# Scaling v by batch: the pair maxima taken apart, and the lanes' maximum through a diagonal and a product of ones

## The chip, the core and the metric

The kernel runs on one core of one Trainium2 chip. Its engines work side by side, each through its own queue in order: TensorE (PE: matmuls, with the weight loads counted apart as PEld), VectorE (DVE), ScalarE (ACT), GpSimd (POOL) and SyncE (SP), which here only issues transfers. The metric is the time of one execution in device microseconds.

## The reference

Causal attention over 8 batches of 8 heads, 576 positions, 64 channels a head, with a bias from cumulative sums; then a feed-forward network (FFN) 512 to 2048 to 512 over all 4608 tokens. q and k come multiplied by 8.

```python
def _attn_ref(q, k, v, s):                      # q, k, v: [8, 8, 576, 64]
    scores = matmul(q, k.transpose(0, 1, 3, 2)) / sqrt(64)
    cum = cumsum(maximum(s, 0), axis=-1)
    bias = -(cum[:, :, :, None] - cum[:, :, None, :])
    scores = where(causal, -1e9, scores + minimum(bias, 0))
    attn = softmax(scores)                      # over the last axis
    return matmul(attn, v)

def _moe_ref(x, w_in, w_out):                   # x: [4608, 512]
    h = x @ w_in                                # [4608, 2048]
    g = where(h >= 1, h, where(h <= -1, 0, (h + 1) ** 2 / 4))
    return g @ w_out
```

## The kernel before, in words

**Tiling.** Heads go in pairs: pair n = 4 * batch + p, with p from 0 to 3. A pair's queries go in two halves, 0 to 319 (query tiles 0 to 2) and 320 to 575 (tiles 3 and 4), and a pair's half is a job. The eight jobs of a batch are the first halves of its four pairs and then the second halves. Tiles are named by pair: `s21_0_1_0` is a score bank of pair 21, tile 0, head 1, from key column 0; `h4_0_9` is block 9 (of 0 to 15) of the FFN's hidden layer for batch 4's first half. Below, "job 19" is the job of pair 19 that the place in question shows.

**A job** has eight slots k. In slot 0 the operands of its scores are made: q and k are split in a high and a low part, Q1s and K1s, Q2s and K2s, by three copies on ScalarE (L392 to L394) and two subtractions on VectorE (L395, L396). These tiles have one buffer each, so a job's operands wait for the scores of the job in front. From slot 2 on come six units of scores: two products on TensorE (L446, L447) into one of two banks of PSUM that all `s` and `px` tiles share, a pass on VectorE (L452: adds the mask, writes p, and keeps the running minimum mn in a second small instruction), and the exponential on ScalarE (L463). The weights are then normalized and split in two float16 parts: sums and reciprocal rs (L502, L503, VectorE), GpSimd (L507, L509, L510), ScalarE (L508), VectorE (L513), and turned by a transposing transfer on SP's queue (L514, pt<-pb). In slot 7 the job in front is finished: thirty products with v into px (L555), and x is split from px by ScalarE (L572) and VectorE (L573).

**FFN steps** of the half whose attention is done (the first half's in a batch's second four jobs, the second half's in the next batch's first four) stand between the slots. A step takes 12 products for a block of h (L614, 320 or 256 columns), ScalarE's evacuation u (L626), two of VectorE (L629, L630), g in two parts (L640 ScalarE, L641 GpSimd), and the products y (L653), two steps later. "FFN products" below are those of L614 and L653.

**Scaling v.** v is loaded a batch ahead into four buffers (`load_v`, slot 1 of the sixth job, of the seventh in the first batch) and scaled by a power of two taken from the batch's largest |v|. `batch_start(b)` finds it: four maxima of 128 x 640 (L295), the maximum of the four (L297), then the maximum over the 128 lanes: a transposing product into a row (L110), VectorE's maximum of the row on one lane (L112), a floor to a power of two in two steps (L95, L96), a cast (L118), a product of ones that spreads it to all lanes (L120), and a copy out of PSUM (L121). A reciprocal and a multiply make rc (L304, L305). GpSimd scales v with rc for each pair of the new batch (L403, slot 1 of the pair's first job); the low part follows on VectorE. Before, `batch_start(b)` is called whole, in slot 5 of the last job of batch b - 1.

**What sets the order.** The Python code gives a program order; a scheduler simulates a timeline and writes each engine's queue from it. `tc.high_priority(offset)` brings instructions forward in its choice (the passes have `TTR_LEAD` = 10000, the FFN's evacuations 6000), and `tc.issue_after(x)` keeps an instruction behind x. So an edit in one place can move others. The first four jobs and the load and split of the weights make the startup, some 130 us in which no steady order holds.

Of the kernel before, what the change touches and what calls it, by code (L numbers as in the profile page):

```python
# [7 lines left out]
BF16 = mybir.dt.bfloat16  # L8
F16 = mybir.dt.float16
F32 = mybir.dt.float32  # L10
# [5 lines left out]
ALU = mybir.AluOpType  # L16
AX = mybir.AxisListType.X
# [3 lines left out]
B, H, S, D = 8, 8, 576, 64  # L21
DM, DFF = 512, 2048
P = 128
NPAIR = H // 2
# [10 lines left out]
TINY = 2.0 ** -50  # L35
# [9 lines left out]
TTR_LEAD = 10000  # L45
# [26 lines left out]

V_K = 5


@with_exitstack
def attention_ffn(ctx: ExitStack, tc: tile.TileContext, qT, kT, vn, s, w_in, w_out, yT):
    nc = tc.nc
    LOADQ, CUMQ, FIRSTQ = nc.sync, nc.scalar, nc.sync
    V, A, G, T = nc.vector, nc.scalar, nc.gpsimd, nc.tensor  # L80

    cp = ctx.enter_context(tc.tile_pool(name="cp", bufs=1))
    ap = ctx.enter_context(tc.tile_pool(name="ap", bufs=2))
    gp = ctx.enter_context(tc.tile_pool(name="gp", bufs=2))
    dp = ctx.enter_context(tc.tile_pool(name="dp", bufs=1, space=DRAM))
    ps_s = ctx.enter_context(tc.tile_pool(name="ps_s", bufs=2, space=PSUM))
    ps_h = ctx.enter_context(tc.tile_pool(name="ps_h", bufs=2, space=PSUM))
# [6 lines left out]
    def pow2floor(out, in_, least):  # L94
        V.tensor_scalar(out, in_, least, None, ALU.max)  # L95
        V.tensor_scalar(out.bitcast(I32), out.bitcast(I32), 0x7F800000, None, ALU.bitwise_and)  # L96

    ident = cp.tile([P, P], F32, name="ident")
# [5 lines left out]
    ones = cp.tile([P, P], BF16, name="ones")  # L104
    G.memset(ones, 1.0)

    def column_max(src, name, bank=(ps_s, "s")):

        row = bank[0].tile([P, 512], F32, tag=bank[1], name=f"row_{name}")
        T.transpose(row[:1, :P], src, ident)  # L110
        top = ap.tile([P, 1], F32, tag="top", name=f"top_{name}")
        V.tensor_reduce(top[:1], row[:1, :P], axis=AX, op=ALU.max)  # L112
        return top[:1]

    def spread(dst, top, name, bank=(ps_s, "s")):

        t16 = ap.tile([P, 1], BF16, tag="t16", name=f"t16_{name}")
        V.tensor_copy(t16[:1], top)  # L118
        col = bank[0].tile([P, 512], F32, tag=bank[1], name=f"col_{name}")
        T.matmul(col[:, :1], ones[:1], t16[:1], start=True, stop=True)  # L120
        V.tensor_copy(dst, col[:, :1])  # L121

    def lane_sum(dst, src, name, tag):

# [157 lines left out]
    vraw, csc, rcs, exs, hsc, rsc, usc, wsc, ubi, gsc, ysc, msc = ({} for _ in range(12))  # L282

    def load_v(b):
        for p in range(NPAIR):
            v = vraw[b, p] = ap.tile([P, NB, P], F32, tag="vraw", bufs=4, name=f"v{b}_{p}")
            G.memset(v[TAIL:, NB - 1], 0.0)
            nc.sync.dma_start(v[:, :NB - 1], vn[b, p, :SP - P].rearrange("(j p) n -> p j n", p=P))
            nc.sync.dma_start(v[:TAIL, NB - 1], vn[b, p, SP - P:])

    def batch_start(b):
        c = ap.tile([P, NPAIR], F32, tag="csc", name=f"c{b}")
        for p in range(NPAIR):
            v = vraw[b, p].rearrange("p j n -> p (j n)")
            V.tensor_reduce(c[:, p:p + 1], v, axis=AX, op=ALU.max, apply_absolute_value=True)  # L295
        t = ap.tile([P, 1], F32, tag="mt", name=f"mt{b}")
        V.tensor_reduce(t, c, axis=AX, op=ALU.max)  # L297
        bank = (ps_h, "h") if b == 1 else (ps_s, "s")
        top = column_max(t, f"m{b}", bank)
        pow2floor(top, top, TINY)  # L300
        m = msc[b] = ap.tile([P, 1], F32, tag="mb", name=f"mb{b}")
        spread(m, top, f"m{b}", bank)
        r = rcs[b] = ap.tile([P, 1], F32, tag="rcs", name=f"rc{b}")
        V.reciprocal(r, m)  # L304
        V.tensor_scalar(r, r, 4096.0, None, ALU.mult)  # L305
# [41 lines left out]
    def plain(n, hf):  # L347
        return jobs.index((n, hf)) < PLAIN_JOBS
# [4 lines left out]
    def att_load(n, hf):  # L353

        b, h0 = n // NPAIR, 2 * (n % NPAIR)
        q0, N, _ = HALF[hf]
        W = q0 + N
        if whole(n, hf):
            for t, src, c0 in zip(operands(n, hf), (qT, kT), (q0, 0)):
                sv = src[b, h0:h0 + 2, :, c0:W].rearrange("h d n -> d h n")  # L360
                (FIRSTQ if jobs.index((n, hf)) < FIRST_N else LOADQ).dma_start(t[:D, :, :W - c0], sv)
            return
        rq = ap.tile([P, 2, N], F32, tag="rq", bufs=1, name=f"rq{n}_{hf}")
        rk = ap.tile([P, 2, W], F32, tag="rk", bufs=1, name=f"rk{n}_{hf}")
        for t, src, c0 in ((rq, qT, q0), (rk, kT, 0)):
            sv = src[b, h0:h0 + 2, :, c0:W].rearrange("h d n -> d h n")
            for d0 in (0, D):
                (FIRSTQ if jobs.index((n, hf)) < FIRST_N else LOADQ).dma_start(t[d0:d0 + D], sv)
        raws[n, hf] = rq, rk

    def att_prep(n, hf):

        q0, N, _ = HALF[hf]
        W = q0 + N
        cd = cumd[2 * n:2 * n + 2].rearrange("h l n -> l h n")
        if not whole(n, hf) and not split_tiles:
            split_tiles.extend(operand_tiles(F32R, "s"))
            constant_rows(*split_tiles[1])
        Qc, Kc = operands(n, hf) if whole(n, hf) else split_tiles[1]
        if jobs.index((n, hf)) < CH_N:  # L380
            for hd in range(2):
                r = ch[2 * n + hd:2 * n + hd + 1]
                CUMQ.dma_start(Qc[D:D + 2, hd, :N].bitcast(F32), r[:, :, q0:W].bitcast(F32))
                CUMQ.dma_start(Kc[D + 2:D + 4, hd, :W].bitcast(F32), r[:, :, :W].bitcast(F32))
        else:
            CUMQ.dma_start(Qc[D:D + 2, :, :N].bitcast(F32), cd[:, :, q0:W])
            CUMQ.dma_start(Kc[D + 2:D + 4, :, :W].bitcast(F32), cd[:, :, :W])
        if whole(n, hf):
            return
        rq, rk = raws.pop((n, hf))  # L390
        (Q1, K1), (Q2, K2) = split_tiles
        A.copy(Q1[:, :, :N], rq)  # L392
        A.copy(K1[:, :, :W], rk)
        A.copy(Q2[:D, :, :N], rq[:D])  # L394
        V.tensor_tensor(Q1[D:, :, :N], rq[D:], Q1[D:, :, :N].bitcast(F32), ALU.subtract)  # L395
        V.tensor_tensor(K2[:D, :, :W], rk[:D], K1[:D, :, :W].bitcast(F32), ALU.subtract)  # L396

    def v_prep(n):

        b, p = n // NPAIR, n % NPAIR  # L400
        v, r = vraw.pop((b, p)), rcs[b]
        VT = vts[n] = ap.tile([P, 2, NB, P], F16, tag="vt", bufs=5, name=f"vt{n}")
        G.tensor_scalar(VT[:, 0], v, r, 1.0, ALU.mult, ALU.mult)  # L403
        if n < V_POOL:
            G.tensor_scalar(v, v, r, 1.0, ALU.mult, ALU.mult)
            G.tensor_tensor(VT[:, 1], v, VT[:, 0], ALU.subtract)
        vbs[n] = VT, v, r

    def v_low(n):
        VT, v, r = vbs.pop(n)  # L410
        if n >= V_POOL:
            with tc.issue_after(ttr[0]):
                V.scalar_tensor_tensor(VT[:, 1], v, r, VT[:, 0], ALU.mult, ALU.subtract)
# [3 lines left out]
    ttr = [None]  # L417
# [157 lines left out]
    jobs = [(NPAIR * b + p, hf) for b in range(B) for hf in range(2) for p in range(NPAIR)]  # L575

    def att_slot(j, k):

        if j < len(jobs):
            n, hf = jobs[j]  # L580
            if k == 0:
                att_prep(n, hf)
            if plain(n, 0):
                if k in (1, 4) and hf == 1 and j < PLAIN_JOBS + 2:
                    v_prep(2 * (j - PLAIN_JOBS) + k // 4)
            elif hf == 0 and k == 1:
                v_prep(n)
            elif hf == 0 and k == V_K:
                v_low(n)
            if k >= 2:  # L590
                scores(n, *UNITS[hf][k - 2])
            if k == 3 and j + 1 < len(jobs):
                att_load(*jobs[j + 1])
            if k == 1 and j % (2 * NPAIR) == V_J + (j < 2 * NPAIR) and j // (2 * NPAIR) + 1 < B:
                load_v(j // (2 * NPAIR) + 1)
            if k == 5 and j + 1 < len(jobs) and jobs[j + 1][0] % NPAIR == 0 and jobs[j + 1][1] == 0:
                with tc.issue_after(ttr[0]):
                    batch_start(jobs[j + 1][0] // NPAIR)
        if k == OUT_K and 1 <= j <= len(jobs) and j != NPAIR:
            while j == len(jobs) and late:  # L600
                late.pop(0)()
            att_out(*jobs[j - 1])
# [109 lines left out]
    c = 0  # L712
    for t in range(8 * NPAIR):
        if t % W1_SLOTS == 0:
            w1_task(c)
            c += 1
        if t == 2:
            load_v(0)
        if t == 6:
            batch_start(0)  # L720
            rc0 = cp.tile([P, 1], F32, name="rc0")
            V.tensor_scalar(rc0, rcs[0], 2.0 ** -10, None, ALU.mult)
        att_slot(t // 8, t % 8)
# [17 lines left out]
    t = 8 * NPAIR  # L741
    for j in range(16 * NP):
# [14 lines left out]
        else:  # L757
# [3 lines left out]
            m = 2 * (j // 8 % 2)  # L761
# [36 lines left out]
```

## Time and profile before

| | us |
|---|---|
| median of three runs | 1073.28 (1072.75 to 1077.13) |
| profiled execution, its own time | 1077.62 |
| its span in the profile | 1075.7, at a mean granted clock of 0.989 |

Each row of the page's first part gives an engine's busy time, its share of the span and its instructions. A row of the stages gives the stretch in us from the span's start, its length, the busy time of PE, PEld, DVE, ACT and POOL with their instructions, the granted TensorE clock, the DMA share and the transfers' rate in GB/s. A row of waits tells who waited <- for which engine's tile and line: us in total, times, longest. A row of the timeline gives start, length, engine, line, operation, output<-inputs, shapes, and how many like instructions it stands for; in brackets how long the engine was idle before it and what ended that. A row with two colons gives the least, median and largest duration in ns, the first and the last start in us, and the shapes.

### The profile page before, as it was taken

How to read it: one execution, taken by the hardware profiler on the slowest of the kernel's cores; microseconds unless marked ns; L12 is line 12 of the kernel's file. 1: busy time of each engine (PE TensorE's matmuls, PEld its weight loads, DVE VectorE, ACT ScalarE, POOL GpSimd, SP SyncE). 2: the span in 40 equal slices, each digit the busy share in tenths (PEclk: the TensorE clock that was granted, in tenths of full speed). 3: DMA queues.
4: the chain of work that ended last, by engine and by line, in shares of the span. 5: the costliest groups of instructions: out<-in, count | busy, mean ns of one | idle time of the engine just before them, and what ended most of it. 6: DMA issues, size and time to landing. Idle time of an engine off the chain costs nothing. (4 is left out here: it accounts for less than half of the span.)

```text
span 1075.7 us, 25023 instructions
## 1 busy us (share of the span) xinstructions
PE 1016.1 (94%) x8539; PEld 780.5 (73%) x8539; DVE 848.5 (79%) x2328; ACT 728.5 (68%) x1707; POOL 650.5 (60%) x1131
## 2 busy tenths in 40 slices
PE   3877899999999999999999999999999999999998
PEld 1444566887777777887778777887778777887787
DVE  6999966687888878888888788888888878887533
ACT  4997965577586756777577756777577756777433
POOL 3744775666666656765576656765576656666422
PEclk9998899999999999999999999999999999999999
DMA  8975535467376754866397765776376654756400
GB/s 248 236 233 136 127 77 126 77 134 149 80 168 133 149 114 110 168 138 142 78 172 140 141 122 104 167 142 136 84 173 142 145 118 90 147 126 130 70 26 20
DMA packets 300839, 140.33 MB, mean 130 GB/s; under 512 B 237608, under 2 KB 286632, under 8 KB 300712
## 3 DMA queue, kind: packets, MB, share of 16 engines
q1 hardware_dynamic: 291008, 128.80, 56.4%
q10 hardware_dynamic: 9704, 9.93, 3.4%
q8 instruction: 67, 1.10, 0.4%
q14 instruction: 60, 0.49, 0.1%
HBM read 71.00 MB, written 9.73 MB: 75 GB/s over the span
## 5 line engine op out<-in xcount | busy, mean ns | idle before, releaser
L614 PE MATMUL h<-x,WI 128*128 128x256 f16 (+1 forms) x3072 | 456.5, 288 | 6.3 <-ACT x L572 2.3
L653 PE MATMUL y<-g,WO 128*128 128x256 f16 (+1 forms) x3072 | 446.9, 287 | 2.5 <-ACT g L640 1.3
L614 PEld LDWEIGHTS <-WI 128*128 128x128 f16 x3072 | 286.4, 98 | 96.7 <-issue 16.0
L653 PEld LDWEIGHTS <-WO 128*128 128x128 f16 x3072 | 286.8, 98 | 86.1 <-issue 7.6
L641 POOL TENSOR_TENSOR g<-u,g 128x320 f16<-128x320 f32 (+1 forms) x256 | 208.5, 815 | 154.7 <-ACT g L640 146.9
L463 ACT ACTIVATE p<-p,mn 64x64 f32<-64x64 f32 (+4 forms) x320 | 179.6, 561 | 107.7 <-DVE mn L452 82.7
L626 ACT ACTIVATE u<-h,ub,us 128x320 f32<-128x320 f32 (+1 forms) x256 | 149.4, 584 | 124.7 <-PE h L614 123.3
L629 DVE SCALAR_TENSOR_TENSOR h<-h,ws,u 128x320 f32<-128x320 f32 (+1 forms) x256 | 132.9, 519 | 91.8 <-ACT u L626 88.6
L507 POOL TENSOR_SCALAR pb<-p,rs 128x256 f16<-128x256 f32 (+4 forms) x148 | 92.3, 623 | 143.3 <-DVE rs L503 92.9
L510 POOL TENSOR_TENSOR pb<-p,pb 128x256 f16<-128x256 f32 (+4 forms) x148 | 156.5, 1057 | 9.9
L452 DVE CUSTOM_DVE_ANT_0 p<-s,mask 64x64 f32<-64x64 f32 (+4 forms) x320 | 134.8, 422 | 30.3 <-PE s L447 17.6
L513 DVE SCALAR_TENSOR_TENSOR pb<-p,rs,pb 128x256 f16<-128x256 f32 (+4 forms) x148 | 128.9, 871 | 23.3 <-POOL pb L507 22.5
L630 DVE SCALAR_TENSOR_TENSOR u<-u,r,h 128x320 f32<-128x320 f32 (+1 forms) x256 | 130.6, 510 | 7.4
L446 PE MATMUL s<-K1s,Q1s 128*128 128x288 f32 (+4 forms) x312 | 117.9, 379 | 10.6 <-DVE mn L452 4.0
L508 ACT ACTIVATE p<-p,rs 128x192 f32<-128x192 f32 (+4 forms) x148 | 84.2, 569 | 49.6 <-DVE rs L503 48.0
L640 ACT CAST g<-u 128x320 f16<-128x320 f32 (+1 forms) x256 | 108.1, 422 | 7.8 <-DVE u L630 7.7
L509 POOL TENSOR_SCALAR pb<-p 128x256 f16<-128x256 f32 (+4 forms) x148 | 87.6, 592 | 23.2 <-ACT p L508 19.2
L447 PE MATMUL s<-K2s,Q2s 68*128 68x288 f32 (+4 forms) x312 | 96.2, 308 | 0.0
L555 PEld LDWEIGHTS <-vt 128*64 128x64 f16 x1464 | 67.8, 111 | 23.0 <-issue 17.6
L555 PE MATMUL px<-pt,vt 128*64 128x256 f16 (+3 forms) x1464 | 77.9, 256 | 5.2 <-DVE mn L452 3.2
L438 POOL MEMSET p<- 128x64 f32 (+1 forms) x320 | 45.2, 158 | 44.0 <-DVE pb L513 21.5
L446 PEld LDWEIGHTS s<-K1s,Q1s 128*128 128x128 f32 (+1 forms) x312 | 56.5, 181 | 20.0 <-PE s L447 4.5
(121 smaller groups left out, 1049.3 us busy)
## 6 DMA issues: line engine op xcount, KB each, us to landing
rk<-in_k_dram SPq DMA_DIRECT2D x56, 288.0 KB
wir<-in_moe_w_in_dram SPq DMA_DIRECT2D x16, 512.0 KB
v<-in_v_dram SPq DMA_DIRECT2D x32, 256.0 KB
wor<-in_moe_w_out_dram SPq DMA_DIRECT2D x16, 512.0 KB
rk<-in_k_dram SPq DMA_DIRECT2D x48, 160.0 KB
rq<-in_q_dram SPq DMA_DIRECT2D x48, 160.0 KB
rq<-in_q_dram SPq DMA_DIRECT2D x56, 128.0 KB
out_dram<-o ACTq DMA_DIRECT2D x32, 160.0 KB
```

The costliest lines, as they stand in the source:

```text
L446: T.matmul(sc[:R, :c1 - c0], Q1[:, hd, qo:qo + R], K1[:, hd, c0:c1], start=True, stop=False)
L452: ttr[0] = V.tensor_tensor_reduce(out=Pt[:R, c0:c1], in0=sc[:R, :c1 - c0], in1=mask[:R, mo:mo + c1 - c0], scale=-0.125, scalar=3.0e38 if m ...
L463: A.activation(Pt[:R, :W], Pt[:R, :W], AF.Exp, bias=m2[:R], scale=-1.0, accum_out=sums[n, i][:R, hd:hd + 1])
L510: G.tensor_tensor(los[1], pw, his[1], ALU.subtract)
L513: V.scalar_tensor_tensor(los[0], pv, rs[:R, :1], his[0], ALU.mult, ALU.subtract)
L555: T.matmul(px[hd * D:(hd + 1) * D, lo:N], vts[n][:, vl, j, hd * D:(hd + 1) * D], PT[:, 4 * j + 2 * hd + pl, lo:], start=(m == 0), stop=(m ...
L614: T.matmul(h[:, :N], WI[4 * kt + ft // 4][:, wl, ft % 4 * P:(ft % 4 + 1) * P], x[:, kt, xl], start=(n == 0), stop=(n == 3 * NKT - 1),)
L626: first = A.activation(u, h[:, :N], AF.Relu, bias=ubi[b], scale=usc[b]).ins
L629: V.scalar_tensor_tensor(h[:, :N], h[:, :N], wsc[b], u, ALU.mult, ALU.max)
L630: V.scalar_tensor_tensor(u, u, r, h[:, :N], ALU.min, ALU.mult)
L641: G.tensor_tensor(g[:, 1], u, g[:, 0], ALU.subtract)
L653: T.matmul(ys[b, hf, m][:, :N], WO[8 * (m // 2) + ft // 2][:, wl, c0:c0 + P], g[:, gl], start=(ft == 0 and n == 0), stop=(ft == NFT - 1 an ...
```

## The change

`batch_start` is taken apart. A new function `pair_max(b, p)` takes one pair's maximum. For batch 1 all four are called in slot 5 of the last job in front, as before; for batches 2 to 7 they are called one at a time in slots 1, 3 and 5 of the seventh job and slot 1 of the eighth. The rest of `batch_start` is called in slot 3 of the eighth job (slot 5 for batch 1), with the passes' priority. The lanes' maximum takes another way: VectorE multiplies the identity by the lanes' values into a diagonal (a 128 x 128 bfloat16 tile), TensorE multiplies a matrix of ones with it, so that every lane gets the row of all 128 values, and VectorE takes the maximum of that row on all lanes. The floor follows on all lanes; transpose, cast and spreading product are gone.

```diff
+PAIR_MAX = ({(7, 5): range(NPAIR)}, {(6, 1): (0,), (6, 3): (1,), (6, 5): (2,), (7, 1): (3,)})
+MAX_AT = ((7, 5), (7, 3))
...
-    def column_max(src, name, bank=(ps_s, "s")):
+    def lane_max(dst, src, name, bank):
+        diag = ap.tile([P, P], BF16, tag="diag", bufs=1, name=f"diag_{name}")
+        V.tensor_scalar(diag, ident, src, None, ALU.mult)
         row = bank[0].tile([P, 512], F32, tag=bank[1], name=f"row_{name}")
-        T.transpose(row[:1, :P], src, ident)
-        top = ap.tile([P, 1], F32, tag="top", name=f"top_{name}")
-        V.tensor_reduce(top[:1], row[:1, :P], axis=AX, op=ALU.max)
-        return top[:1]
-
-    def spread(dst, top, name, bank=(ps_s, "s")):
-        t16 = ap.tile([P, 1], BF16, tag="t16", name=f"t16_{name}")
-        V.tensor_copy(t16[:1], top)
-        col = bank[0].tile([P, 512], F32, tag=bank[1], name=f"col_{name}")
-        T.matmul(col[:, :1], ones[:1], t16[:1], start=True, stop=True)
-        V.tensor_copy(dst, col[:, :1])
+        T.matmul(row[:, :P], ones, diag, start=True, stop=True)
+        V.tensor_reduce(dst, row[:, :P], axis=AX, op=ALU.max)
...
+    def pair_max(b, p):
+        if p == 0:
+            csc[b] = ap.tile([P, NPAIR], F32, tag="csc", name=f"c{b}")
+        v = vraw[b, p].rearrange("p j n -> p (j n)")
+        V.tensor_reduce(csc[b][:, p:p + 1], v, axis=AX, op=ALU.max, apply_absolute_value=True)
+
     def batch_start(b):
-        c = ap.tile([P, NPAIR], F32, tag="csc", name=f"c{b}")
-        for p in range(NPAIR):
-            v = vraw[b, p].rearrange("p j n -> p (j n)")
-            V.tensor_reduce(c[:, p:p + 1], v, axis=AX, op=ALU.max, apply_absolute_value=True)
         t = ap.tile([P, 1], F32, tag="mt", name=f"mt{b}")
-        V.tensor_reduce(t, c, axis=AX, op=ALU.max)
-        bank = (ps_h, "h") if b == 1 else (ps_s, "s")
-        top = column_max(t, f"m{b}", bank)
-        pow2floor(top, top, TINY)
+        V.tensor_reduce(t, csc.pop(b), axis=AX, op=ALU.max)
         m = msc[b] = ap.tile([P, 1], F32, tag="mb", name=f"mb{b}")
-        spread(m, top, f"m{b}", bank)
+        lane_max(m, t, f"m{b}", (ps_h, "h") if b == 1 else (ps_s, "s"))
+        pow2floor(m, m, TINY)
...
-            if k == 5 and j + 1 < len(jobs) and jobs[j + 1][0] % NPAIR == 0 and jobs[j + 1][1] == 0:
+            b = j // (2 * NPAIR) + 1
+            for p in PAIR_MAX[b > 1].get((j % (2 * NPAIR), k), ()) if b < B else ():
                 with tc.issue_after(ttr[0]):
-                    batch_start(jobs[j + 1][0] // NPAIR)
+                    pair_max(b, p)
+            if b < B and (j % (2 * NPAIR), k) == MAX_AT[b > 1]:
+                with tc.issue_after(ttr[0]), tc.high_priority(offset=TTR_LEAD):
+                    batch_start(b)
```

In the changed kernel's rows the attention's line numbers are five lower (L447 is the pass that was L452, L441 and L442 the scores that were L446 and L447, L390 was L395, L508 was L513) and the FFN's one lower (L613 was L614, L628 and L629 were L629 and L630, L652 was L653); L290 is the pair's maximum. A pass shows as two rows, `ISA p<-s,mask` and `ISA mn`.

VectorE at the boundary from batch 4 to 5, before: the block of four maxima (c5 is the batch's tile of maxima, v5_0 to v5_3 the raw v of its pairs), with the last pass of head 0 in job 19 ahead.

```order
L452 ISA p19_4_0_9421,mn19_4_0_288_9452<-s19_4_0_288_9449,mask_84,mn19_4_0_0_9426 128x288
L452 ISA mn19_4_0_288_9452 128x1
L295 TENSOR_REDUCE c5_9455<-v5_0_8838 128x1
L295 TENSOR_REDUCE c5_9455<-v5_1_8842 128x1
L295 TENSOR_REDUCE c5_9455<-v5_2_8846 128x1
L295 TENSOR_REDUCE c5_9455<-v5_3_8850 128x1
```

The maxima follow one another, with no pass or evacuation between them. After, on VectorE in job 18, the last two maxima:

```order
L447 ISA p18_4_0_9164,mn18_4_0_288_9195<-s18_4_0_288_9192,mask_84,mn18_4_0_0_9169 128x288
L447 ISA mn18_4_0_288_9195 128x1
L290 TENSOR_REDUCE c5_9071<-v5_2_8826 128x1
L447 ISA p18_4_1_9215,mn18_4_1_0_9220<-s18_4_1_0_9217,mask_84 128x288
L447 ISA mn18_4_1_0_9220 128x1
L628 SCALAR_TENSOR_TENSOR h4_0_6_9428<-h4_0_6_9428,ws4_8556,u4_0_6_9441 128x320
L629 SCALAR_TENSOR_TENSOR u4_0_6_9441<-u4_0_6_9441,r4_8546,h4_0_6_9428 128x320
L447 ISA p18_4_1_9215,mn18_4_1_288_9244<-s18_4_1_288_9241,mask_84,mn18_4_1_0_9220 128x288
L447 ISA mn18_4_1_288_9244 128x1
L290 TENSOR_REDUCE c5_9071<-v5_3_8830 128x1
```

Each maximum stands behind a pass now, about a job earlier, with two passes and an evacuation between the third and the fourth. TensorE in job 21, before, with two scores of tiles 0 and 1 and what follows (WI12 is a block of the first weight, x4_1 the second half of batch 4's x):

```order
L446 MATMUL s21_0_1_0_9903<-K1s_2619,Q1s_2618 64x64
L447 MATMUL s21_0_1_0_9903<-K2s_2621,Q2s_2620 64x64
L446 MATMUL s21_1_0_0_9939<-K1s_2619,Q1s_2618 128x192
L447 MATMUL s21_1_0_0_9939<-K2s_2621,Q2s_2620 128x192
L614 LDWEIGHTS WI12_122
```

The two scores follow one another. The same place after:

```order
L441 MATMUL s21_0_1_0_9879<-K1s_2611,Q1s_2610 64x64
L442 MATMUL s21_0_1_0_9879<-K2s_2613,Q2s_2612 64x64
L613 LDWEIGHTS WI12_122
L613 MATMUL h4_1_0_10058<-x4_1_9029,WI12_122 128x256
L613 LDWEIGHTS WI12_122
L613 MATMUL h4_1_0_10058<-x4_1_9029,WI12_122 128x256
L652 LDWEIGHTS WO15_141
L652 MATMUL y4_0_3_9202<-g4_0_12_9826,WO15_141 128x320
```

FFN products have come between the first of these scores and the second. VectorE at the operands of job 23 (rq23_0 and rk23_0 are its raw q and k, pb22_1 the weights of job 22's tile 1), before:

```order
L452 ISA p22_2_1_10286,mn22_2_1_0_10291<-s22_2_1_0_10288,mask_84 128x320
L452 ISA mn22_2_1_0_10291 128x1
L513 SCALAR_TENSOR_TENSOR pb22_1_10232<-p22_1_0_10194,rs22_1_10233,pb22_1_10232 128x2x128
L395 TENSOR_TENSOR Q1s_2618<-rq23_0_10163,Q1s_2618 64x640
L396 TENSOR_TENSOR K2s_2621<-rk23_0_10164,K1s_2619 64x2x320
```

The split of pb22_1 stands between job 22's last pass and the operands. After:

```order
L508 SCALAR_TENSOR_TENSOR pb22_1_10208<-p22_1_0_10170,rs22_1_10209,pb22_1_10208 128x2x128
L629 SCALAR_TENSOR_TENSOR u4_1_6_10441<-u4_1_6_10441,r4_8546,h4_1_6_10428 128x256
L447 ISA p22_2_1_10262,mn22_2_1_0_10267<-s22_2_1_0_10264,mask_84 128x320
L447 ISA mn22_2_1_0_10267 128x1
L390 TENSOR_TENSOR Q1s_2610<-rq23_0_10139,Q1s_2610 64x640
```

The split has moved ahead of an evacuation and of that pass, and the operands follow the pass.

More of the change, by code (lines that the diff above doesn't have):

```diff
@@ L719, in attention_ffn @@
         if t == 6:
+            for p in range(NPAIR):
+                pair_max(0, p)
             batch_start(0)
```

## The prediction

> **What bounds the kernel now.** I read the page's first part, then the busy time by stage, then TensorE's waits after the startup, then the timelines of one batch boundary on every engine. The times below are of the boundary from batch 4 to 5, where job 20 (pair 20, queries 0 to 319) is the first of the new batch; jobs 18 and 19 are here the second halves of those pairs, the last two of the old.
>
> ```profile
> PE 1016.1 (94%) x8539; PEld 780.5 (73%) x8539; DVE 848.5 (79%) x2328; ACT 728.5 (68%) x1707; POOL 650.5 (60%) x1131
> 584.00:648.00 64.00, 64.00 (x535) 48.69 (x533) 51.52 (x130) 41.14 (x89) 37.83 (x58) 1.00 0.66 130
> 648.00:712.00 64.00, 61.49 (x587) 50.95 (x585) 53.45 (x163) 47.73 (x128) 45.27 (x92) 1.00 0.69 144
> PE s L446 <- DVE mn L452: 4.0, 6, 0.7
> PE s L446 <- ACT Q2s L394: 2.3, 2, 1.2
> PE h L614 <- ACT x L572: 2.3, 5, 0.5
> PE s L446 <- DVE Q1s L395: 2.2, 2, 1.1
> PE s L446 <- ACT x L572: 2.2, 2, 1.4
> PE px L555 <- DMA pt<-pb: 2.0, 3, 0.9
> PE y L653 <- ACT g L640: 1.3, 6, 0.2
> PE y L653 <- POOL g L641: 0.2, 1, 0.2
> ```
>
> TensorE is the bound: full in the stretch up to the boundary, 2.51 us idle in the one behind it. The waits are all that TensorE had between 200 and 1032 us (total, times, longest): 16.5 us. The sixes are the six boundaries to batches 2 to 7. Their places:
>
> ```profile
> 665.09 1.51 PE L555 MATMUL px<-pt,vt 128*64 128x256 f16 x30
> 668.07 0.38 PE L614 MATMUL h<-x,WI 128*128 128x256 f16 x2 [0.46 <-ACT x L572]
> 669.20 0.33 PE L446 MATMUL s<-K1s,Q1s 128*128 128x192 f32 x1 [0.66 <-DVE mn L452]
> 670.87 1.25 PE L653 MATMUL y<-g,WO 128*128 128x320 f16 x8 [0.21 <-ACT g L640]
> 690.09 0.21 PE L446 MATMUL s<-K1s,Q1s 128*64 128x64 f32 x1 [1.18 <-ACT Q2s L394]
> 667.09 0.56 ACT L508 ACTIVATE p<-p,rs 128x320 f32<-128x320 f32 x1 [0.74 <-DVE rs L503]
> 667.56 0.46 ACT L572 ACTIVATE x<-px,shares_wi 128x256 f16<-128x256 f32 x1
> 688.12 0.61 DVE L513 SCALAR_TENSOR_TENSOR pb<-p,rs,pb 128x256 f16<-128x256 f32 x1 [0.98 <-POOL pb L507]
> 688.76 1.18 DVE L395 TENSOR_TENSOR Q1s<-rq,Q1s 64x640 fp32r<-64x640 f32 x1
> ```
>
> Four waits, 2.5 us: x of the old batch's last pair (0.46), a score bank (0.66), g (0.21), and the operands of job 23 (1.18). The third is short; the last ends with Q1s's low half on VectorE, which queued behind a split (L513) that waited for GpSimd. All lie 25 to 50 us behind the maxima:
>
> ```profile
> L295 DVE TENSOR_REDUCE c<-v x32: 802/803/820, 13.9 to 882.7; 128x1 f32<-128x640 f32 x32
> 637.91 2.99 DVE L295 TENSOR_REDUCE c<-v 128x1 f32<-128x640 f32 x4
> 637.47 0.62 ACT L626 ACTIVATE u<-h,ub,us 128x320 f32<-128x320 f32 x1 [1.51 <-PE h L614]
> 640.82 0.54 DVE L629 SCALAR_TENSOR_TENSOR h<-h,ws,u 128x320 f32<-128x320 f32 x1
> 642.21 1.79 PE L614 MATMUL h<-x,WI 128*128 128x320 f16 x12
> 646.21 0.40 PE L446 MATMUL s<-K1s,Q1s 128*128 128x288 f32 x1
> 647.53 2.35 POOL L403 TENSOR_SCALAR vt<-v,rc 128x640 f16<-128x640 f32 x3 [1.60 <-DVE rc L305]
> ```
>
> The block of 2.99 us makes an evacuation (L629) start 2.7 us after ScalarE was done at 638.09, yet TensorE's next h (642.21) has no wait: the block costs nothing where it stands. What it does is to push the attention behind the FFN.
>
> **The change, part by part.** *Order.* In the order shown with the change, VectorE's block at the boundary is gone, and the same four reductions stand one by one in jobs 18 and 19, each beside a score's pass or an evacuation of h. With it TensorE's own order moves. Between the scores s19_4_0_288 and s19_4_1_0 (the product at 646.21) stood 71 FFN products, now 4, counted in the two orders; job 20's first score comes some 33 FFN products earlier, job 21's some 25. One FFN product takes 0.15 us with 320 columns (1.79 / 12 in the row of 642.21), and I estimate 0.12 us with 256 by the ratio of columns, so the lead is 3 to 5 us. What was late at the boundary gets this lead. In job 21 TensorE had two scores back to back, the second being the one that waited 0.66 us for the pass of an earlier score to clear its bank; now 14 FFN products stand between them, which is 14 x 0.12 = 1.7 us of cover.
>
> The first wait: from job 19's px (665.09 + 1.51 = 666.6) to the first product on the last x stood 7 FFN products, now 26, about 3 us; and ScalarE forms x ahead of L508 (now L503) instead of behind its 0.74 us wait. Both kinds go: 2.3 + 4.0 in the table of waits, all six boundaries together. The fourth: at job 23's operands the split that waited 0.98 us for GpSimd stood ahead of Q1s on VectorE; now the split stands ahead of an evacuation and the last pass of job 22, and Q1s follows the pass. So Q1s can start when ScalarE's half is there, over 1 us sooner, and the cover between job 22's last score and job 23's first grows from 18 FFN products to 25 (7 x 0.12 = 0.8 us). Together that exceeds 1.18 us, so the three rows of waits for Q2s, Q1s and the x that delays them go too: 2.3 + 2.2 + 2.2 = 6.7 us. I keep the waits for g (1.3) and for transposes (2.0), which nothing here touches. Off: 2.3 + 4.0 + 6.7 = 13.0 us.
>
> *The maxima in their new places* move 24 x 0.803 = 19.3 us of VectorE work. No DMA goes with them, so SP's and GpSimd's queues are as before. What is queued behind each is an evacuation or a score's pass, for which TensorE waits. Their cover is VectorE's idle time in jobs 18 and 19, in the brackets here:
>
> ```profile
> 610.77 0.56 DVE L629 SCALAR_TENSOR_TENSOR h<-h,ws,u 128x320 f32<-128x320 f32 x1 [2.17 <-ACT u L626]
> 621.15 1.11 DVE L513 SCALAR_TENSOR_TENSOR pb<-p,rs,pb 128x512 f16<-128x512 f32 x1 [0.47 <-POOL pb L507]
> 624.53 0.52 DVE L452 CUSTOM_DVE_ANT_0 p<-s,mask,mn 128x288 f32<-128x288 f32 x1 [0.40 <-PE s L447]
> 630.38 0.56 DVE L629 SCALAR_TENSOR_TENSOR h<-h,ws,u 128x320 f32<-128x320 f32 x1 [1.36 <-ACT u L626]
> ```
>
> That is 2.17 + 0.47 + 0.40 + 1.36 = 4.4 us of idle time for 4 x 0.80 = 3.2 us of work, and since 2.7 us of lateness at once passed unfelt in the block, 0.8 us should too. The ends are 0 (all covered) and 19.3 (none); the nearest row is the block's, which cost nothing, so I charge 1.0. v itself is loaded a batch ahead, so no DMA is waited for.
>
> *The lanes' maximum.* Out go three VectorE steps, a transposing product and a broadcast product; in come a 128x128 multiply and a maximum over 128 lanes.
>
> ```profile
> L112 DVE TENSOR_REDUCE top_m<-row_m x8: 271/272/278, 20.1 to 885.5; 1x1 f32<-1x128 f32 x8
> L118 DVE CAST t_m<-top_m x8: 140/144/144, 21.8 to 886.2; 1x1 bf16<-1x1 f32 x8
> 646.31 0.16 DVE L121 COPY mb<-col_m 128x1 f32<-128x1 f32 x1 [0.36 <-PE col_m L120]
> 653.24 0.47 DVE L573 SCALAR_TENSOR_TENSOR x<-px,shares_wi,x 128x256 f16<-128x256 f32 x1
> ```
>
> Removed are 0.27 + 0.14 + 0.16 = 0.57; the power-of-two floor runs on 128 lanes now, one element in each as before, and keeps its two steps. The maximum has L112's length: 0.27. The multiply lies between L118 (one element) and L573 (256 wide): 0.14 to 0.47, and I take 0.27, as L112 is also 128 wide. Net 0. The new maximum waits for one product instead of two waits for products (0.36 in the row); behind it on VectorE stand an evacuation and a score's pass. Bounds per boundary: 0.36 less, or 1.4 more if the product is late by its own 0.27 and eight y products (1.1); inside the unfelt 2.7 either way. GpSimd's 1.60 us before vt ends sooner, off the path: nothing.
>
> *Startup.* VectorE's queue is reordered up to 130 us.
>
> ```profile
> PE px L555 <- DVE mn L452: 3.2, 1, 3.2
> 95.00:100.00 5.00, 3.18 (x6) 1.15 (x5) 4.50 (x17) 5.00 (x10) 0.80 (x1) 0.50 0.92 209
> 110.00:115.00 5.00, 4.03 (x32) 3.29 (x33) 5.00 (x12) 4.98 (x9) 2.87 (x4) 0.50 0.99 205
> 115.00:120.00 5.00, 5.00 (x19) 2.72 (x18) 4.89 (x11) 3.85 (x7) 2.34 (x4) 0.51 0.74 190
> ```
>
> The px wait of 3.2 us ends at about 111 us. The pass that it hung on moves from place 283 to 272 of VectorE's queue, but the first evacuation of h from 261 to 268. I take half the wait: -1.5. The ends are -7.7 (below), and +3.2 if the wait doubles.
>
> **Sum.** -13.0 + 1.0 - 1.5 = -13.5 us, from the profiled execution's 1077.62 to 1064.1; that execution is 4.3 above the median of 1073.28, which goes to 1059.8.
>
> **Rivals.** *The waits come back elsewhere.* Q1s, K1s, Q2s, K2s have one buffer; each job must wait for the last score and then for about 3 us of copies. If that is the limit, an order with more cover in one place has less in another (between job 21's operands and its first score stood 16 FFN products, now 10). Against it: most jobs show no wait. Half of 13.0 comes back, startup 0: about 1068 to 1075, say 1072. Perfetto Trace Analysis (Optimization Strategy) of the Trainium skill reads the same gap repeating on the engine that should be full as a possible lack of buffers, which would be this rival; the 0.66 us wait for a score bank agrees, the 0.74 us on L508 does not.
>
> *Slower: the scattered maxima reach TensorE.* Place: the four 0.80 us reductions ahead of passes and evacuations in jobs 18 and 19. It decides from 0.56 us each (13.5 / 24). At full price with half of the waits gone: +19.3 - 6.5 = +12.8, 1086. For it: only 0.47 and 0.40 idle at two of the spots.
>
> *The startup's clock.* The three 5 us rows have the granted clock at 0.50 around TensorE's gaps. If the 3.2 us wait goes whole and the 9.0 us of work at 110 to 120 run at full clock: -3.2 - 4.5 = -7.7, 1053. TensorE: Matmul & The Clock Gate (The two states you'll see) of the Trainium skill has the clock halved after an idle window of about 3.4 us; by that rule this rival holds if the gap is cut, and the rows agree so far.
>
> **How the numbers follow.** Main case 0.60 (1054 to 1066), waits elsewhere 0.20, slower 0.08, startup's clock 0.12. The predicted time is the main case's, 1060. The range from 1052 to 1075 leaves out the slower case and some edges. A difference under 0.5% (5.4 us) a measurement can't tell. Faster: 0.60 + 0.12 + 0.02 of the second = 0.74; same 0.17; slower 0.09.
>
> **What would show it.** Right: TensorE full behind the boundaries, with no "s <- Q2s", "s <- Q1s" or "s <- mn" there, and under 4 us of waits between 200 and 1030 us; the new multiply 0.2 to 0.3 us; no TensorE wait at the four maxima. Wrong: waits "s <- mn" or "h <- u" in the last two jobs of a batch (slower), "s <- Q1s" in its second job (waits elsewhere), or a wait "px <- mn" at about 110 us of 3.2 us or more (startup not better).

## The result, and the profile after

The changed kernel takes 1057.1 us in the median of six runs (1056.77 to 1058.29), the kernel before beside it 1073.78 (six runs, 1072.59 to 1081.6): a ratio of 0.9832, interval 0.9803 to 0.9862. Timed again later it came to 0.9847 (0.9823 to 0.9871). It is faster by 15 to 17 us; 1060 was predicted. The profiled execution took 1058.29 us, with a span of 1056.5 and a mean granted clock of 0.969. Ratios are of fast executions alone; of all those below only one was slow, 2043.0 us with the maxima doubled.

The first part of the page after, the two stretches that answer to those shown of before (the boundary from batch 4 to 5 falls some 9 us earlier now), and all that TensorE waited for between 200 and 1032 us:

```profile
PE 1011.8 (96%) x8531; PEld 782.0 (74%) x8531; DVE 846.8 (80%) x2320; ACT 726.3 (69%) x1707; POOL 646.9 (61%) x1131
575.00:639.00 64.00, 64.00 (x556) 49.29 (x554) 54.99 (x144) 43.56 (x96) 38.81 (x60) 1.00 0.65 132
639.00:703.00 64.00, 64.00 (x602) 53.58 (x597) 53.27 (x155) 47.16 (x127) 44.79 (x91) 1.00 0.61 144
PE px L550 <- DMA Q2s<-cumd: 0.4, 1, 0.4
PE y L652 <- POOL g L640: 0.3, 1, 0.3
```

Both stretches are full, and of 16.5 us of waits 0.7 are left. The same boundary on TensorE and ScalarE:

```profile
652.38 1.51 PE L550 MATMUL px<-pt,vt 128*64 128x256 f16 x30
653.91 1.53 PE L652 MATMUL y<-g,WO 128*128 128x320 f16 x10
655.28 1.15 PE L613 MATMUL h<-x,WI 128*128 128x256 f16 x9
659.50 0.34 PE L441 MATMUL s<-K1s,Q1s 128*128 128x192 f32 x1
660.11 1.26 PE L652 MATMUL y<-g,WO 128*128 128x320 f16 x8
654.26 0.47 ACT L567 ACTIVATE x<-px,shares_wi 128x256 f16<-128x256 f32 x1
655.41 0.56 ACT L503 ACTIVATE p<-p,rs 128x320 f32<-128x320 f32 x1 [0.68 <-DVE rs L498]
```

No row of TensorE carries a bracket any more. ScalarE forms x ahead of its waiting step L503, and ten y products stand behind px before the next h. The new steps on VectorE, and a spread maximum:

```profile
618.66 0.82 DVE L290 TENSOR_REDUCE c<-v 128x1 f32<-128x640 f32 x1
627.63 0.27 DVE L113 TENSOR_SCALAR diag_m<-ident,mt 128x128 bf16<-128x128 f32 x1
630.41 0.28 DVE L116 TENSOR_REDUCE mb<-row_m 128x1 f32<-128x128 f32 x1
```

Full rows also tell less than the whole saving. Below is one batch period of each kernel, cut to hold 1059 TensorE instructions, and then the stretch from 200 to 1032 us, each before and then after:

```profile
552.70:673.80 121.10, 118.59 (x1059) 93.78 (x1058) 99.62 (x275) 84.05 (x205) 78.48 (x141) 1.00 0.67 133
546.10:663.50 117.40, 117.40 (x1059) 93.70 (x1058) 99.52 (x275) 83.76 (x206) 76.67 (x142) 1.00 0.64 139
200.00:1032.00 832.00, 815.38 (x7250) 642.77 (x7249) 670.05 (x1826) 567.40 (x1366) 525.43 (x928) 1.00 0.62 128
200.00:1032.00 832.00, 831.04 (x7449) 662.13 (x7448) 676.89 (x1842) 575.04 (x1389) 532.48 (x942) 1.00 0.59 129
```

The period shrank by 3.70 us, of which 2.51 were idle time in the profile; 1.19 us more went out of the busy time itself, for as many instructions. The longer stretch agrees: an instruction takes 0.1125 us of TensorE's busy time on average before and 0.1116 after, at a granted clock of 1.00 in both, which over 7449 instructions makes some 7 us.

The startup went the other way. The stretches 40 to 60 and 60 to 80 us, before and then after, and the two gaps of TensorE in the first of them, after:

```profile
40.00:60.00 20.00, 17.64 (x65) 10.92 (x64) 18.84 (x55) 18.29 (x42) 12.26 (x20) 1.00 0.82 231
60.00:80.00 20.00, 14.57 (x49) 8.08 (x49) 20.00 (x58) 19.68 (x40) 8.43 (x16) 1.00 0.72 222
40.00:60.00 20.00, 12.21 (x58) 7.69 (x58) 18.26 (x52) 18.29 (x36) 9.54 (x17) 0.70 0.62 177
60.00:80.00 20.00, 16.80 (x58) 9.54 (x55) 19.91 (x57) 19.57 (x43) 8.58 (x14) 0.50 0.64 205
49.94 1.12 PE L475 MATMUL pp<-ident,p 128*128 128x128 f32 x4 [3.31 <-ACT pt L476]
54.18 1.65 PE L438 MATMUL s<-K2w,Q2w 68*128 68x192 f32 x4 [3.12 <-DVE mn L447]
```

TensorE does 5.4 us less in the first stretch, and its clock falls to 0.50 in the second.

### The profile page after: what moved, and what is told of

The parts are those of the page before. It is cut to its first block, busy times and chain, and to the rows that moved or that the text cites. A ratio compares the mean times of both kernels' runs of the same rounds, so it can differ in the third digit from the quotient of the medians.

```text
span 1056.5 us, 24915 instructions
## 1 busy us (share of the span) xinstructions
PE 1011.8 (96%) x8531; PEld 782.0 (74%) x8531; DVE 846.8 (80%) x2320; ACT 726.3 (69%) x1707; POOL 646.9 (61%) x1131
## 4 chain that ended last, share of the span: by engine, by line
PE 85%; DVE 4%; DMA 2%; ACT 2%; issue 1%; POOL 1%; SPq 0%; DVEq 0%; ACTq 0%; POOLq 0%
PE y L652 35%; PE h L613 34%; PE px L550 7%; PE s L441 4%; PE s L442 4%; PE s L438 1%; DMA wor<-in_moe_w_out_dram 1%; DVE pb L508 1%; DMA pt<-pb 1%; DVE p L447 1%; ACT p L458 0%; DVE h L628 0%; ACT wor L221 0%; DVE WO L225 0%; DMA K1w<-in_k_dram 0%
## 5 line engine op out<-in xcount | busy, mean ns | idle before, releaser
L613 PE MATMUL h<-x,WI 128*128 128x256 f16 (+1 forms) x3072 | 462.7, 289 | 1.3 <-DVE x L568 0.7
L652 PE MATMUL y<-g,WO 128*128 128x256 f16 (+1 forms) x3072 | 448.5, 287 | 0.9 <-POOL g L640 0.8
L613 PEld LDWEIGHTS <-WI 128*128 128x128 f16 x3072 | 286.2, 99 | 90.4 <-issue 9.2
L652 PEld LDWEIGHTS <-WO 128*128 128x128 f16 x3072 | 286.9, 98 | 83.2 <-issue 8.6
L640 POOL TENSOR_TENSOR g<-u,g 128x320 f16<-128x320 f32 (+1 forms) x256 | 204.6, 799 | 134.9 <-ACT g L639 134.4
L628 DVE SCALAR_TENSOR_TENSOR h<-h,ws,u 128x320 f32<-128x320 f32 (+1 forms) x256 | 132.5, 518 | 82.3 <-ACT u L625 81.4
L447 DVE CUSTOM_DVE_ANT_0 p<-s,mask 64x64 f32<-64x64 f32 (+4 forms) x320 | 134.2, 421 | 56.3 <-PE s L442 36.3
L505 POOL TENSOR_TENSOR pb<-p,pb 128x256 f16<-128x256 f32 (+4 forms) x148 | 150.8, 1019 | 10.3
L508 DVE SCALAR_TENSOR_TENSOR pb<-p,rs,pb 128x256 f16<-128x256 f32 (+4 forms) x148 | 138.6, 937 | 15.8 <-POOL pb L502 15.0
L629 DVE SCALAR_TENSOR_TENSOR u<-u,r,h 128x320 f32<-128x320 f32 (+1 forms) x256 | 130.3, 509 | 6.7
L441 PE MATMUL s<-K1s,Q1s 128*128 128x288 f32 (+4 forms) x312 | 118.2, 381 | 0.1
L503 ACT ACTIVATE p<-p,rs 128x192 f32<-128x192 f32 (+4 forms) x148 | 84.5, 571 | 44.0 <-DVE rs L498 42.6
L442 PE MATMUL s<-K2s,Q2s 68*128 68x288 f32 (+4 forms) x312 | 96.5, 310 | 0.0
L504 POOL TENSOR_SCALAR pb<-p 128x256 f16<-128x256 f32 (+4 forms) x148 | 90.0, 608 | 5.5 <-ACT p L503 3.4
L441 PEld LDWEIGHTS s<-K1s,Q1s 128*128 128x128 f32 (+1 forms) x312 | 56.9, 182 | 8.1 <-DVE mn L447 0.3
```

The source lines that it names most:

```text
L441: T.matmul(sc[:R, :c1 - c0], Q1[:, hd, qo:qo + R], K1[:, hd, c0:c1], start=True, stop=False)
L442: T.matmul(sc[:R, :c1 - c0], Q2[:KC, hd, qo:qo + R], K2[:KC, hd, c0:c1], start=False, stop=True)
L447: ttr[0] = V.tensor_tensor_reduce(out=Pt[:R, c0:c1], in0=sc[:R, :c1 - c0], in1=mask[:R, mo:mo + c1 - c0], scale=-0.125, scalar=3.0e38 if m ...
L505: G.tensor_tensor(los[1], pw, his[1], ALU.subtract)
L508: V.scalar_tensor_tensor(los[0], pv, rs[:R, :1], his[0], ALU.mult, ALU.subtract)
L613: T.matmul(h[:, :N], WI[4 * kt + ft // 4][:, wl, ft % 4 * P:(ft % 4 + 1) * P], x[:, kt, xl], start=(n == 0), stop=(n == 3 * NKT - 1),)
```

## The experiments

The change has two parts that can be had apart: the maxima spread over two jobs, and the lanes' maximum through the diagonal. Theory O: the order that the scheduler writes for TensorE pays, and the block of maxima costs nothing where it stands. Theory V: relieving VectorE of the block pays. Theory S: the startup pays. Ratios are to the kernel before on the same chip, with 95% intervals. Where a run is called "old startup", batches 0 and 1 keep the old way to the lanes' maximum, and the startup is ordered nearly as before.

**The diagonal alone** (block in its old place).

```diff
...
-        top = column_max(t, f"m{b}", bank)
-        pow2floor(top, top, TINY)
...
-        spread(m, top, f"m{b}", bank)
+        lane_max(m, t, f"m{b}", (ps_h, "h") if b == 1 else (ps_s, "s"))
+        pow2floor(m, m, TINY)
...
```

> The kernel before with the lanes' maximum through the diagonal alone; the four maxima stay one block in the old place. Theory O (the order written for TensorE is what pays; the block on VectorE costs nothing): TensorE's queue here has a part of the lead (55 FFN products between the scores s19_4_0_288 and s19_4_1_0 against 71 before and 4 in the changed kernel; job 20's first score 19 products earlier; still only 1 product between job 21's two scores), so a part of the six boundaries' waits goes: the x wait (0.46 each) yes, the score bank's 0.66 no, job 23's part: 1064 to 1070 us. Theory V (what pays is that the block of 2.99 us no longer holds VectorE): the block is still there, so 1072 to 1075. Theory S (the startup pays, since the new chain for batch 0 reorders it): 1060 or less with the boundary waits unchanged.

Measured: 1065.61 us, 0.9899 (0.9880 to 0.9919). V and S fall: the block is where it was, and the gain is here. But the score bank's wait went too, which O had kept.

**The spread alone** (the changed kernel with the old way to the lanes' maximum; the diff above in reverse).

> The changed kernel with the old way to the lanes' maximum (transpose, one lane's maximum, cast, product of ones, copy); the four maxima spread and the rest called in slot 3 as in the changed kernel. The startup is that of before. Theory O: TensorE's lead is small here (job 20's first score 2 products earlier than before, job 21's second score 4 products behind the first, job 23's 32 behind job 22's last), so the x wait of 0.46 stays, the bank's 0.66 falls by the 0.5 us of 4 products, the 1.18 at job 23 goes: about 9 us of waits less, 1062 to 1067. Theory V: the block is gone, so all of it: 1056 to 1059. Theory S: the startup is the old one, so 1071 to 1075.

Measured: 1071.82 us, 0.9953 (0.9935 to 0.9971). V is refuted a second time: the block is gone, and 5 us are gained. The time lies in the range of S, which the runs before and behind it rule out. O's number was missed too; new waits stand in place of the old ones between 200 and 1032 us, the largest of them here:

```profile
PE y L662 <- POOL g L650: 4.0, 5, 0.8
PE s L451 <- DVE mn L457: 3.2, 8, 0.9
```

**The changed kernel with the old startup.**

```diff
...
-        lane_max(m, t, f"m{b}", (ps_h, "h") if b == 1 else (ps_s, "s"))
...
+        if b < 2:
+            top = column_max(t, f"m{b}", bank)
...
+        else:
+            lane_max(m, t, f"m{b}", bank)
...
-                with tc.issue_after(ttr[0]), tc.high_priority(offset=TTR_LEAD):
+                with tc.issue_after(ttr[0]), tc.high_priority(offset=TTR_LEAD if b > 1 else 0):
...
```

The last two lines give the call for batch 1 its old priority back.

> The changed kernel, but batches 0 and 1 take the old way to the lanes' maximum: the order from batch 2 on is that of the changed kernel, the order of the first 130 us nearly that of before. Theory O: the boundary waits are gone as in the changed kernel; only the startup's share comes back, 0.5 to 3.5 us: 1057.5 to 1061. Theory S: 1065 or more. Theory V: as O.

Measured: 1053.81 us, 0.9793 (0.9773 to 0.9813), less than expected, and S falls here too. The steady part gains 2.1%, about 22 us. That is more than the changed kernel's 0.9832, though the two intervals overlap; what the new startup costs is measured further below.

**The diagonal from batch 2 on, alone**, which takes the startup out of the first run.

> The kernel before with the lanes' maximum through the diagonal from batch 2 on; startup, block of maxima and places as before. If the run with the diagonal everywhere (0.9899) lost about 4 us in its startup, this one is at 1058 to 1062: some 15 us from the way to the lanes' maximum alone, with under 5 us of waits from 200 to 1030 us. If the startup was no loss there, 1064 to 1067.

Measured: 1061.97 us, 0.9864 (0.9839 to 0.9889). All that TensorE waits for between 200 and 1032 us:

```profile
PE px L567 <- DMA pt<-pb: 1.6, 2, 1.4
PE y L665 <- ACT g L652: 1.3, 5, 0.5
PE h L626 <- DVE u L642: 0.7, 1, 0.7
PE y L665 <- POOL g L653: 0.6, 2, 0.4
```

So with the old startup throughout, the spread gives 0.5% (5 us), the diagonal 1.4% (15 us), both 2.1% (22 us).

**The startup alone**: the kernel before with the diagonal in batches 0 and 1 only.

> The kernel before with the new way to the lanes' maximum in batches 0 and 1 alone: the startup is that of the changed kernel, all else as before. If the startup's order costs what the changed kernel and the run with the old startup differ by (0.9832 to 0.9793): 3 to 6 us slower than before, 1078 to 1081 against 1075. By the recorded prediction's term: 1.5 us faster, 1073 to 1074.

Measured: 1079.21 us, 1.0030 (1.0013 to 1.0047), 3.2 us slower, at the lower edge of what was expected. Its two gaps are those of the changed kernel, but in its profiled execution the clock stayed at 1.00 there:

```profile
50.26 1.12 PE L492 MATMUL pp<-ident,p 128*128 128x128 f32 x4 [2.85 <-ACT pt L493]
54.70 1.65 PE L455 MATMUL s<-K2w,Q2w 68*128 68x192 f32 x4 [3.33 <-DVE mn L464]
60.00:80.00 20.00, 17.13 (x62) 9.79 (x61) 19.91 (x56) 19.61 (x44) 8.58 (x14) 1.00 0.67 211
```

The first output leaves TensorE no sooner for that: its evacuation starts at 171.2 us here and at 171.6 in the changed kernel at half clock (169.9 in a second execution, also at half clock; 166.3 before). The kernel with the old startup also had 0.50 from 60 to 80 us, and a gap of 3.78 us near 56 us, and its first output starts at 165.1. So neither the clock there nor gaps of that size near 50 us explain the loss. A likelier place is later, where TensorE's rows here and then before are these:

```profile
101.05 1.33 PE L455 MATMUL s<-K2w,Q2w 68*128 68x288 f32 x2 [4.58 <-DVE mn L464]
108.39 3.71 PE L626 MATMUL h<-x,WI 128*128 128x320 f16 x24
100.12 3.10 PE L614 MATMUL h<-x,WI 128*128 128x320 f16 x12 [1.34 <-DVE u L630]
103.55 1.79 PE L614 MATMUL h<-x,WI 128*128 128x320 f16 x12
```

In the new order a score stands ahead of the two blocks of h and waits 4.58 us for a pass; before, the two blocks came first, some 7 us sooner. The changed kernel has the same wait, at 100.39 us. That this wait makes the whole 3.2 us was not tested.

**One bank.** The product of ones writes into the row's bank instead of taking a second one from the scores; all steps of the old way stay, and the block too.

```diff
...
-        col = bank[0].tile([P, 512], F32, tag=bank[1], name=f"col_{name}")
-        T.matmul(col[:, :1], ones[:1], t16[:1], start=True, stop=True)
-        V.tensor_copy(dst, col[:, :1])
+        T.matmul(col[:, P:P + 1], ones[:1], t16[:1], start=True, stop=True)
+        V.tensor_copy(dst, col[:, P:P + 1])
...
-        spread(m, top, f"m{b}", bank)
+        spread(m, top, f"m{b}", row)
...
```

> The kernel before with one edit: the product of ones that spreads the lanes' maximum writes into a column of the bank that the transposed row has, instead of taking a second score bank. All steps of the old way stay (transpose, maximum on one lane, floor, cast, product, copy), and the block too. Theory B (what the diagonal brought is that it takes one score bank instead of two in turn, so that the scores behind are ordered earlier): as the run with the diagonal from batch 2 on, 1057 to 1063. Theory C (what it brought is the shorter chain, one product and one way back instead of two): nearly as before, 1070 to 1076.

Measured: 1070.61 us, 0.9946 (0.9924 to 0.9968), some 9 us short of the diagonal. Theory B falls as it stood; C gave about the right number, but the next run takes its reason away.

**Spread and one bank together**: still the old chain of steps, but TensorE's order comes near the changed kernel's.

> The run with the maxima spread and the old way to the lanes' maximum (0.9953), with its product of ones written into the row's bank. All the steps of the old way stay on the engines. The order written for TensorE comes near the changed kernel's by this (job 20's first score 31 products earlier than before, job 21's 26; 17 products between s21_0_1 and s21_1_0, 30 ahead of job 23). Theory O (TensorE's order carries the gain, whatever chain brings it about): 1052 to 1058, under 3 us of waits from 200 to 1030 us. Theory C (the shorter chain itself carries it on the engines): as the run with the spread alone, 1068 to 1072.

Measured: 1053.91 us, 0.9798 (0.9776 to 0.9819), as good as the changed kernel with the old startup. TensorE's waits from 200 to 1032 us are these:

```profile
PE y L661 <- POOL g L649: 1.2, 2, 0.6
PE px L559 <- DMA pt<-pb: 0.4, 1, 0.4
```

No part of the diagonal is needed on the engines: the old chain in another order has the whole steady gain. That is the test between O and C, and it goes to O. What in the order carries the gain is not isolated by it, as no run changed TensorE's order and nothing else.

**Small maxima**: the kernel before with the reductions of batches 2 to 7 over 8 columns.

```diff
             v = vraw[b, p].rearrange("p j n -> p (j n)")
+            v = v if b < 2 else v[:, :8]
```

> The kernel before with the four maxima of batches 2 to 7 taken over 8 of 640 columns, so that most of their work is left out (the scale is then the maximum of fewer values): places and chain stay, VectorE loses 16 us or more. Theory V (the block is what cost): 1056 to 1060. Theory O: only what the order moves by itself (65 products instead of 71 between s19_4_0_288 and s19_4_1_0, job 20's start 3 later, 32 instead of 18 ahead of job 23), so 1066 to 1074.

Measured: 1071.69 us, 0.9961 (0.9944 to 0.9977). Taking nearly all of the block's work away gives 4 us, what the moved order alone was to give.

**Doubled maxima** (changed kernel, old startup; each reduction of batches 2 to 7 is written twice).

> The changed kernel with the old startup, and each of the 24 spread maxima taken twice: 19.3 us more work on VectorE in the same places; TensorE's order stays nearly the same (27 FFN products instead of 25 ahead of job 23, 98 and 288 at the jobs' starts unchanged). Theory O (covered by VectorE's idle time, since TensorE has its cover in the order): 1053 to 1057. Theory of the slower rival (what stands behind each maximum is late and TensorE feels it): up to 1073, with waits s <- mn or h <- u in the last two jobs of a batch.

Measured: 1054.2 us, 0.9796 (0.9771 to 0.9821), against 0.9793 without the doubling. The 24 added reductions are there, and yet VectorE's busy time is the same (849.0 against 848.4 us); first its rows with the doubling (the second maximum is L308), then without:

```profile
L308 DVE TENSOR_REDUCE c<-v 128x1 f32<-128x640 f32 x24 | 19.4, 809 | 0.1
L532 DVE SCALAR_TENSOR_TENSOR pb<-p,rs,pb 128x256 f16<-128x256 f32 (+4 forms) x148 | 121.1, 818 | 17.1 <-POOL pb L526 16.2
L530 DVE SCALAR_TENSOR_TENSOR pb<-p,rs,pb 128x256 f16<-128x256 f32 (+4 forms) x148 | 140.1, 946 | 15.8 <-POOL pb L524 14.8
```

The splits of the weights took 19.0 us less as the maxima added 19.4; why they did is not shown.

**The block early** (changed kernel, old startup): all four maxima in slot 1 of the seventh job.

```diff
-PAIR_MAX = ({(7, 5): range(NPAIR)}, {(6, 1): (0,), (6, 3): (1,), (6, 5): (2,), (7, 1): (3,)})
+PAIR_MAX = ({(7, 5): range(NPAIR)}, {(6, 1): range(NPAIR)})
```

> The changed kernel with the old startup, and the four maxima of batches 2 to 7 called as one block in slot 1 of the seventh job instead of one by one. Theory O/B (it is enough that the lanes' maximum leaves the scores' banks early; how the maxima are spread is nothing): 1052 to 1056. Theory V (a block of 3.2 us in one piece costs): 1060 or more, with TensorE waiting for VectorE behind the block, about 1 us or more each time.

Measured: 1054.01 us, 0.9793 (0.9769 to 0.9818). One block or four pieces is the same within the intervals.

**Another bank**: the kernel before, with the two small products in a bank of h in every batch but the first.

```diff
-        bank = (ps_h, "h") if b == 1 else (ps_s, "s")
+        bank = (ps_h, "h") if b else (ps_s, "s")
```

> The kernel before with one edit: the two small products of the lanes' maximum take their PSUM bank from the two of h instead of the two that the scores share, in every batch but the first. Block of maxima, chain and places are as before. The order written gives the scores more lead than the changed kernel (12 FFN products between s19_4_0_288 and s19_4_1_0, job 20's first score 148 products earlier than before). Theory O, with the reason that the chain held a score bank and so put the scores behind: the boundary waits go, 1057 to 1061 with the startup of before, or up to 1066 if h now waits 1 us at each boundary for the bank that the chain holds. Theory V: the block is still there in one piece, 1072 to 1075.

Measured: 1116.79 us, 1.0381 (1.0360 to 1.0403), 41 us slower; both theories are far off. At the same boundary, VectorE, GpSimd and TensorE:

```profile
655.87 5.48 DVE L513 SCALAR_TENSOR_TENSOR pb<-p,rs,pb 64x128 f16<-64x128 f32 x1
661.38 0.36 DVE L452 CUSTOM_DVE_ANT_0 p<-s,mask 128x192 f32<-128x192 f32 x1
656.38 2.34 POOL L403 TENSOR_SCALAR vt<-v,rc 128x640 f16<-128x640 f32 x3
659.82 1.39 POOL L510 TENSOR_TENSOR pb<-p,pb 128x640 f16<-128x640 f32 x1
661.41 0.15 POOL L438 MEMSET p<- 128x64 f32 x1 [0.21 <-DVE pb L513]
661.80 0.41 PE L446 MATMUL s<-K1s,Q1s 128*128 128x320 f32 x1 [3.32 <-DVE mn L452]
663.58 1.76 PE L614 MATMUL h<-x,WI 128*128 128x320 f16 x6 [1.21 <-DVE u L630]
```

A split of 64 x 128 lasts 5.48 us while GpSimd works without a pause, and ends just behind GpSimd's first pause; the pass behind it comes late, and TensorE waits 3.32 us for it. Such a split of 5.5 to 6.4 us stands at each of the six boundaries; in the steady part of the other kernels none is over 2.2 us. Behind the wait TensorE's granted clock falls:

```profile
660.00:664.00 4.00, 0.99 (x4) 0.65 (x5) 4.00 (x11) 1.50 (x5) 2.74 (x5) 0.79 0.00 0
664.00:668.00 4.00, 4.00 (x16) 2.21 (x15) 3.94 (x15) 3.27 (x8) 2.07 (x5) 0.50 1.04 200
```

Between 200 and 1032 us TensorE's waits come to 36.8 us, 20 more than before. The mean clock there is 0.98, and an instruction takes 0.1150 us of busy time against 0.1125, which over 6911 instructions is another 17. These two make most of the 41; how much of them hangs on the splits was not tested. More lead for the scores is thus not better by itself.

**The changed kernel again**, beside the startup alone.

> The changed kernel as it is, on the same chip as the run with the new startup alone. If the startup is a loss of 3 to 6 us, this one is at 1055 to 1060, 3 to 6 us above the run with the old startup (1053.8).

Measured: 1060.65 us, 0.9847 (0.9823 to 0.9871), at the upper edge of what was expected. The kernel with the old startup (up to 0.9813) is faster than the kernel before, and than this one by its second timing (the interval of the first, from 0.9803, still touches); so are the block early and the spread with one bank, which cannot be told from one another.

## Why the prediction was right, and where it was not

The time was right in part by luck, a sum of two errors of opposite sign: the steady part gave 22 us where 12 were predicted, and the startup lost 3 where a gain of 1.5 was predicted.

*The waits at the boundaries.* Right in place and cause: the 0.46, 0.66 and 1.18 us waits are gone, and in the order that was read, before the run, as the carrier. The term of 13.0 us was too small. The waits for g and for transposes, which it kept (3.3 us), went as well, as they seem to hang on the same order; and each period lost 1.19 us that the profile had booked as busy, about 7 us over six boundaries, as the rows from 200 to 1032 us show too. With 15.8 us of idle time this makes some 22 to 23; the runs with the old startup measured 22. Which instructions held the 1.19 us stays open; waits shorter than the modelled end of a matmul would be booked so, but no run tested it.

*What moves the order.* The failed step is the sentence that the block pushes the attention behind the FFN, and the costing of the lanes' maximum at net 0. With nearly all of the block's work left out, only 4 us were gained. On VectorE the new steps take the predicted 0.27 and 0.28 us, but the order hung on them more than on the spread: 15 us with the diagonal alone, 5 with the spread alone. The count of products in job 21 was read too narrowly as well: with the diagonal alone only one product stands between the two scores, and the wait is gone. With two banks, what sets a bank free is the pass of the score before the last, so the products ahead of that score count too.

*The maxima in their places.* 1.0 us was charged; doubling them costs nothing that can be measured (0.9796 against 0.9793), so the term is 0 within the intervals, and the slower rival is refuted: its point of decision was 0.56 us for each maximum, and 0.8 more for each was not felt.

*The startup.* 1.5 us of gain were predicted, 3.2 us of loss measured: the wrong sign. Of the px wait of 3.2 us 0.4 is left (1.3 in a second execution), so more is gone than the half that was to go. But a score's wait of 4.58 us came in its place some 10 us earlier, ahead of two blocks of h. The prediction had counted that the first evacuation of h moves back in VectorE's queue, from place 261 to 268, and gave that no price. The rival on the clock falls too: from 110 to 120 us the clock did rise in the changed kernel (1.00 and 0.98 in the two rows of 5 us that had 0.50 and 0.51), and the startup lost nonetheless. The 0.50 stands at 100 to 105 us now. By the page TensorE: Matmul & The Clock Gate (The two states you'll see) of the Trainium skill, the clock is halved after an idle window of about 3.4 us, and the window runs freely. The trace differs: in the changed kernel the clock is at 0.50 from 48.2 us on, 1.6 us into the gap of 3.31 us, and in the startup alone a gap of 3.33 us did not lower it. No run here shows the window itself.

*Waits that come back elsewhere.* They do not in the steady part of the changed kernel (0.7 us left). This rival describes its startup, and the spread alone, where 4.0 us for g and 3.2 us for passes stand in place of what went.

## What to carry to other kernels

When a scheduler writes the queues, a small edit is first an edit of the order: build each part alone, read how many products stand between a result and its use, and time the parts before crediting one, as the count alone did not tell which part would gain. A reduction on an engine with idle time is priced by doubling it, not by its length. Look at the startup apart from the steady part, as one chain used in both can gain in one and lose in the other. A full row of TensorE does not mean that nothing is left: divide its busy time by its instructions as well.

## What the runs showed of the hardware

A split on VectorE can last many times its usual length while GpSimd works: 64 x 128 in 5.48 us, beside eight GpSimd instructions in a row from 655.68 to 661.21 us (the rows above are some of them), where the 28 of that shape in the kernel with the old startup average 0.44 us. GpSimd paused only because its next step waited for that very split (0.21 us, in the row of 661.41). The page SBUF — State Buffer of the Trainium skill (SBUF: two separate sides) has a pair of ports that VectorE and GpSimd share, locked for the whole of one instruction, the other engine blocked, where the VectorE instruction has two inputs in SBUF and the GpSimd one reads it. The trace agrees on the blocking, but here VectorE stayed blocked over several GpSimd instructions, until the first pause. The five forms of the split together took 121.1 us in one kernel and 140.1 in another with the same splits; what makes that difference was not tested.

TensorE's busy time in the profile holds time that a better order saves, as said above: 0.1125 us for an instruction before and 0.1116 after, at a granted clock of 1.00. And its clock can halve soon after its last product: 1.6 us behind it in the changed kernel's startup, at 48.2 us.
